# One unbroken TensorE run for two attention tiles, and stores issued by ScalarE, in a fused attention and two-layer FFN kernel

## The chip, the cores and the metric

One core of one Trainium2 chip runs the whole program. The metric is the device time of the program in microseconds (us), the median of three runs. TensorE (PE in the profile) multiplies, VectorE (DVE), ScalarE (ACT) and GpSimd (POOL) work on elements, SyncE (SP) issues transfers. A transfer is issued by an instruction of one engine's queue and then runs on the core's 16 DMA engines.

## The reference

Three stages follow each other. Lengths: 4 sequences of 768 tokens, 8 heads of 64, so 3072 tokens of width 512.

```
for c in range(768 // 32):                       # chunks of 32 queries
    k_ctx = k[32c-16 : 32c+40], clipped;  k_full = [8 memory keys, k_ctx];  the same for v
    a = softmax(q_c @ k_full.T / 8)              # the maximum is subtracted, 1e-9 added to the sum
    out_c = a @ v_full
x = out as 3072 x 512
h = x @ w_in;  g = h - tanh(h);                      x = g @ w_out     # first FFN, 512 -> 2048 -> 512
h = x @ w_in;  g = max(h, 0) + alpha * min(h, 0);  out = g @ w_out     # second FFN
```

The FFN weights arrive as 64-bit floats, everything else as 32-bit.

## The kernel before, in words

**Tiles, blocks and slots.** The 3072 tokens are 24 tiles of 128. Each FFN layer goes through 6 blocks of 4 tiles (512 columns), and each block through 16 slots, one for each 128 of the 2048 inner features. A slot is 24 matmuls of 128x512: twelve that make `h` (`emit_h`, L173) and twelve that add to the four `y` banks (`emit_y`; L212 in the first layer, L217 in the second). Twelve, since every operand is held as a high and a low part and three of the four products are taken. Between the two stands `emit_g`: in the first layer a tanh on ScalarE (L188), a subtraction on VectorE (L189), the high part on ScalarE (L197) and the low part on GpSimd (L198). TensorE works ahead: `h` of later slots is multiplied before `y` of this one.

**Attention inside the first layer.** The first five tiles get their scores before the first block, and their values mostly there too. Each later tile goes through its steps between the FFN matmuls of the first layer: `emit_scores` (16 matmuls into the bank `sp`, L301, then maximum, subtraction, exponential), `emit_soft` (sum, division, transposition, copies into `ebuf`), `tok_c`, which calls `emit_pv` (16 matmuls of `ebuf` with the values `vn` into the bank `pv`, L353, then two copies into `ring`, from where the FFN reads its input). The trace has two records for each of these 16 matmuls, so 32 for a tile's scores and 32 for its values. A dictionary `plan` sets at which half slot of which block each step is emitted: position 2f before `emit_y` of slot f, 2f+1 after it. `SPACE`, `PERIOD`, `LC`, `LP` and `SLACK` shape it. So scores of tile 5 stand at position 8 of block 0, those of tiles 6, 7 and 8 at 14, 21 and 33, and a tile's values five positions behind its scores.

**Who decides the order.** The program gives every step as an instruction stream, and a scheduler then reorders instructions on each engine, by its own model, as long as dependencies hold. `tc.issue_after(ins)` adds one edge: what is emitted under it stays behind `ins` on that engine. Before the change, only single places have such an edge. The scheduler therefore cuts the runs of `sp` and `pv` matmuls and puts FFN matmuls between the pieces.

**Buffers.** PSUM has four banks for `y`, two for `h` and two (`ps_a`) that `sp`, `pv` and the weight conversion `u` share. In SBUF, four buffers `t` are shared by tanh results, converted weights `s` and the block's results `ys`; `kbuf`, `qn` and `vn` have one buffer each for a later tile.

**Block 0 and the weights.** In block 0 each slot also converts two weight matrices of the first layer from 64 to 32 bits (`to_f32`: ScalarE L96, VectorE L99, L102, L106) and splits them. In blocks 1 to 4 the second layer's weights are converted and written to DRAM (`park`), and in block 5 they are read back (`unpark`), all by transfers that SyncE issues.

**Block ends.** `evac_y` copies the four `y` banks into four buffers `ys`, two copies by ScalarE (L233) and two by VectorE (L235), and issues four stores to `y1d` (first layer) or `out` (second), before the change all on SyncE's queue (L236). Since `ys` takes all four `t` buffers, the next tanh waits until a store has landed.

Of the kernel before, what the change touches and what calls it, by code (L numbers as in the profile page):

```python
# [17 lines left out]
L_CTX, R_CTX, CH, NM, SEQ = 16, 8, 32, 8, 768  # L18
NEG = -1.0e30
PERIOD = 20  # L20
LC, LP, SLACK = 5, 3, 2
SPACE = 6
SCB = 2
FIRST = 1
# [12 lines left out]
def chunk_attention_two_ffn_kernel(  # L37
# [128 lines left out]
    def emit_h(l, b, n, f):  # L166
        wi = wts[l, f][0]
        s0 = x0[l][b]
        h = ps_h.tile([128, 512], FP32, tag="h", name="h")[:, :n * 128]
        i = 0  # L170
        for kk in range(KD):
            for a, c in PASS:
                mm = nc.tensor.matmul(  # L173
                    out=h, lhsT=wi[:, a, kk, :], rhs=ring[c][:, s0:s0 + n, kk, :],
                    start=(i == 0), stop=(i == 3 * KD - 1),
                )
                i += 1
        last["h"] = mm.ins
        hp[l, b, f] = h

    def emit_g(l, b, n, f):
# [19 lines left out]
    def emit_y(l, b, n, f):  # L201
        wo = wts[l, f][1]
        g = gs.pop((l, b, f))
        m = KD if l == 0 else n
        if f == 0:
            yp[l, b] = [ps_y.tile([128, 512], FP32, tag="y", name="y") for _ in range(m)]
        order = ((0, 0), (1, 0), (0, 1)) if l == 0 else ((0, 0), (0, 1), (1, 0))
        for a, c in order:
            for j in range(m):
                first, last = f == 0 and (a, c) == order[0], f == NF - 1 and (a, c) == order[-1]  # L210
                if l == 0:
                    nc.tensor.matmul(  # L212
                        out=yp[l, b][j][:, :n * 128], lhsT=wo[:, a, j * 128:(j + 1) * 128],
                        rhs=g[c], start=first, stop=last,
                    )
                else:
                    nc.tensor.matmul(  # L217
                        out=yp[l, b][j], lhsT=g[a][:, j * 128:(j + 1) * 128],
                        rhs=wo[:, c, :], start=first, stop=last,
                    )  # L220

    def evac_y(l, b, n, t0):
        ys = yp.pop((l, b))
        for j, y in enumerate(ys):
            if l == 0:
                s = t_p.tile([128, 512], FP32, tag="t", name="ys")[:, :n * 128]
                src, dst = y[:, :n * 128], y1d[t0:t0 + n, :, j, :].rearrange("i p c -> p i c")
                so = s.rearrange("p (i c) -> p i c", i=n)
            else:
                s = t_p.tile([128, 512], FP32, tag="t", name="ys")  # L230
                src, dst, so = y, out[(t0 + j) * 128:(t0 + j + 1) * 128, :], s
            if j % 2 == 0:
                nc.scalar.activation(out=s, in_=src, func=ACTF.Copy)  # L233
            else:
                nc.vector.tensor_copy(out=s, in_=src)  # L235
            nc.sync.dma_start(out=dst, in_=so)  # L236

    x2 = {}

# [46 lines left out]
    def load_v(t):  # L286
        if t < NS:
            vt[t] = w_p.tile([KW, 2, H * D], FP32, tag="w", name="vn")
        else:
            vt[t] = ac.tile([KW, 2, H * D], FP32, tag="v", name="vn", bufs=1)  # L290
        nc.sync.dma_start(out=vt[t], in_=v[t])
# [3 lines left out]
    def emit_scores(t):  # L295
        s = t % TPS
        kn = kt.pop(t)
        sp = ps_a.tile([128, 512], FP32, tag="a", name="sp")
        for p in range(HP):
            for c in range(4):  # L300
                nc.tensor.matmul(  # L301
                    out=sp[CH * c:CH * c + CH, 128 * p:128 * p + 128],
                    lhsT=qt[t][:, p, CH * c:CH * c + CH],
                    rhs=kn[p // 2][:, :, p % 2, c // 2, CH * (c % 2):CH * (c % 2) + W + NM],
                    start=True, stop=True,
                )
        sp = sp.rearrange("q (h n) -> q h n", h=H)
        if s == 0:
            nc.vector.memset(sp[0:CH, :, 0:L_CTX], NEG)
        if s == TPS - 1:  # L310
            nc.vector.memset(sp[128 - CH:128, :, 64 - R_CTX:64], NEG)
        sc = aw.tile([128, H, 64], FP32, tag="sc", name="sc", bufs=SCB)
        mx = aw.tile([128, H, 1], FP32, tag="mx", name="mx")
        mb = mx.to_broadcast([128, H, 64])
        if t < SUB_POOL:
            nc.scalar.activation(out=sc, in_=sp, func=ACTF.Copy)
            nc.vector.tensor_reduce(out=mx, in_=sp, op=ALU.max, axis=AX.X)
            nc.gpsimd.tensor_tensor(out=sc, in0=sc, in1=mb, op=ALU.subtract)
        else:
            nc.vector.tensor_reduce(out=mx, in_=sp, op=ALU.max, axis=AX.X)  # L320
            nc.vector.tensor_tensor(out=sc, in0=sp, in1=mb, op=ALU.subtract)
        last["exp"] = nc.scalar.activation(out=sc, in_=sc, func=ACTF.Exp, scale=scale).ins
        sm[t] = sc
# [22 lines left out]
    def emit_pv(t, slot):  # L346
        pool, tag = (ps_h, "h") if t < NS else (ps_a, "a")
        pv = pool.tile([128, 512], FP32, tag=tag, name="pv")
        for p in range(HP):
            for a in range(2):  # L350
                for j in range(2):
                    h = 2 * p + j
                    nc.tensor.matmul(  # L353
                        out=pv[D * j:D * j + D, 128 * p + 64 * a:128 * p + 64 * a + 64],
                        lhsT=vt[t][:, a, D * h:D * h + D],
                        rhs=ebuf[:, a, h, :],
                        start=True, stop=True,
                    )
        pvv = pv.rearrange("k (p n) -> k p n", p=HP)
        nc.scalar.activation(out=ring[0][:, slot], in_=pvv, func=ACTF.Copy)  # L360
        nc.vector.tensor_tensor(
            out=ring[1][:, slot], in0=pvv, in1=f32(ring[0][:, slot]), op=ALU.subtract
        )
# [21 lines left out]
    def tok_c(t):  # L385
        b, i = first_of[t]
        if t == NS:
            with tc.issue_after(last["h"]):
                emit_pv(t, x0[0][b] + i)
        else:  # L390
            emit_pv(t, x0[0][b] + i)
        if NS < t + 1 < NTILE:
            load_v(t + 1)

    slots = [(0, b, n, f) for b, n in enumerate(blocks1) for f in range(NF)]
    slots += [(1, b, n, f) for b, n in enumerate(blocks2) for f in range(NF)]
# [2 lines left out]
    if True:  # L399
# [38 lines left out]
        def release(t):  # L438
            b, i = first_of[t]
            prev = max([x for x in range(b) if not (  # L440
                x0[0][x] + blocks1[x] <= x0[0][b] + i or x0[0][x] > x0[0][b] + i)], default=None)
            return 0 if prev is None else base[prev] + 2 * NF - 1

        def per(g):
            return PERIOD / dur[min(max(0, int(g)) // (2 * NF), len(dur) - 1)]

        at = {}
        g = 1e9
        for t in reversed(range(n0 + 1, NTILE)):
            g = min(base[first_of[t][0]] - 4 - LC, g - per(g))  # L450
            at[t] = g
        pos = -4
        todo = []
        for t in range(n0 + 1, NTILE):
            lo = max(pos + (SPACE if t > n0 + 1 else 0), 0, release(t) - LC, release(t - 1) - 2)
            pos = at[t] = max(lo, int(at[t]) - SLACK)
        for t in range(n0, NTILE):
            a = at.get(t, -4)
            nxt = at.get(t + 1, 1e9)
            c = max(min(a + LC, nxt + 2), release(t), 0)  # L460
            assert c <= base[first_of[t][0]] - 3, (t, c)
            if t > n0:
                todo.append((a, 10 * t, emit_scores, t))
                todo.append((a + 2, 10 * t + 3, emit_soft, t))
            if t > n0 and t + 1 < NTILE:
                todo.append((max(a + 1, nxt - LP), 10 * t + 1, loads_to, t + 1))
            todo.append((c, 10 * t + 12, tok_c, t))
        for a, _, fn, t in sorted(todo, key=lambda x: x[:2]):
            plan.setdefault(a, []).append((fn, t))
        nc.sync.dma_start(out=alpha_sb, in_=alpha.rearrange("(k p) -> p k", p=128))  # L470
        emit_h(*slots[0])
        emit_g(*slots[0])
        for i, (l, b, n, f) in enumerate(slots):
            def attn(pos):
                if l == 0:
                    for fn, t in plan.pop(base[b] + pos, []):
                        fn(t)

            if l == 0 and b == 0:
                more_w()  # L480
# [12 lines left out]
                if f == XF:  # L493
                    split_x2(0, blocks2[0])
            if i + 1 < len(slots):
                emit_h(*slots[i + 1])
                emit_g(*slots[i + 1])
            attn(2 * f)
            emit_y(l, b, n, f)
            if f == NF - 1:  # L500
                evac_y(l, b, n, (start1 if l == 0 else start2)[b])
            attn(2 * f + 1)
            if l == 1 and b + 1 < len(blocks2):
                if f == 2:
                    load_x2(b + 1, blocks2[b + 1], start2[b + 1])
# [63 lines left out]
```

## Time and profile before

| what | value |
|---|---|
| three runs | 1165.69, 1167.29, 1168.5 us; median 1167.29 us |
| the profiled execution | 1164.67 us, its span 1162.9 us |
| PE busy | 1125.7 us, 97% of the span |
| DVE, ACT, POOL busy | 42%, 30%, 31% |
| PE h L173, y L212, y L217 in the chain that ended last | 42%, 20%, 22% of the span |
| PE sp L301, pv L353 in that chain | 2% and 2% |

How to read it: a row of the timeline is a run of like instructions with its start, its time and the idle time before it. A matmul's record reaches past the start of the next one, because matmuls overlap; what a run takes from TensorE is therefore the time from its start to the start of the next run. A bracket at the end tells how long the engine had been idle and what it had waited for.

### The profile page before, as it was taken

Reading aid. Unit: us, or ns where it says so; the run is one execution under the profiler, and the core shown is the slowest. Engines: PE = TensorE matmul, PEld = TensorE weight load, DVE = VectorE, ACT = ScalarE, POOL = GpSimd, SP = SyncE. Lnnn points to the kernel's source line nnn. Section 1 sums busy time; section 2 is a strip of 40 time slices with the busy share of each in tenths; the row PEclk is TensorE's granted clock in tenths of the full one; section 3 lists DMA queues with packets and bytes.
Section 4 is the critical chain, followed back from the end, with each engine's and each line's share of the span. In section 5 each row is a group of like instructions: output and inputs, shape, how many; then the busy total and the mean of one; then the engine's idle time right before and its main releaser. Section 6 shows DMA issues by size and latency. Waiting matters only on the chain.

```text
span 1162.9 us, 15549 instructions
## 1 busy us (share of the span) xinstructions
PE 1125.7 (97%) x6144; PEld 914.2 (79%) x6144; DVE 488.9 (42%) x806; ACT 344.4 (30%) x612; POOL 362.9 (31%) x299
## 2 busy tenths in 40 slices
PE   3799999999999999999899999999999999999998
PEld 3587777878787777778788888888888888888886
DVE  6888645545445554454112323323323223322222
ACT  4556543434334443344222112112112112111111
POOL 4565533323333333333222222222222222222221
PEclk9799999999999999999999999999999999999999
DMA  9664244344344444335655101100101000000000
GB/s 274 221 233 143 73 144 134 123 149 128 123 145 146 133 140 149 128 123 175 221 196 186 37 1 37 37 1 37 37 1 37 37 1 1 37 1 5 33 1 36
DMA packets 53688, 112.16 MB, mean 96 GB/s; under 512 B 7280, under 2 KB 25712, under 8 KB 53616
## 3 DMA queue, kind: packets, MB, share of 16 engines
q1 hardware_dynamic: 53616, 111.18, 29.3%
q8 instruction: 48, 0.79, 0.3%
q14 instruction: 24, 0.20, 0.1%
HBM read 81.80 MB, written 29.36 MB: 96 GB/s over the span
## 4 chain that ended last, share of the span: by engine, by line
PE 89%; DVE 5%; issue 2%; DMA 2%; ACT 1%; SPq 1%; POOL 0%; DVEq 0%; POOLq 0%; ACTq 0%
PE h L173 42%; PE y L217 22%; PE y L212 20%; PE sp L301 2%; PE pv L353 2%; DVE u L102 1%; DVE s L106 1%; DVE u L99 1%; DMA w2d<-pk 1%; DMA kbuf<-in_k_dram 1%; DMA y1d<-ys 0%; DVE ebuf L344 0%; SPq L275 0%; ACT wt L112 0%; DVE et L335 0%
## 5 line engine op out<-in xcount | busy, mean ns | idle before, releaser
L173 PE MATMUL h<-ring,wt 128*128 128x512 f32 x2304 | 561.8, 392 | 12.2 <-DVE t L189 9.4
L173 PEld LDWEIGHTS h<-ring,wt 128*128 128x128 f32 x2304 | 432.1, 189 | 107.1 <-DVE t L189 11.1
L198 POOL TENSOR_TENSOR gl<-t,gh 128x512 fp32r<-128x512 f32 x192 | 248.8, 1296 | 615.6 <-ACT gh L197 585.6
L197 ACT ACTIVATE gh<-t 128x512 fp32r<-128x512 f32 x192 | 121.0, 630 | 462.3 <-DVE t L194 412.4
L191 DVE TENSOR_SCALAR t<-h,alpha_sb 128x512 f32<-128x512 f32 x96 | 72.1, 751 | 341.6 <-PE h L173 332.2
L212 PE MATMUL y<-gh,wt 128*128 128x512 f32 x768 | 195.0, 395 | 0.0
L217 PE MATMUL y<-wt,gh 128*128 128x512 f32 x768 | 191.6, 389 | 0.0
L217 PEld LDWEIGHTS y<-wt,gh 128*128 128x128 f32 x768 | 144.1, 188 | 30.0
L212 PEld LDWEIGHTS y<-gh,wt 128*128 128x128 f32 x768 | 141.6, 188 | 32.4 <-issue 2.6
L189 DVE TENSOR_TENSOR t<-h,t 128x512 f32<-128x512 f32 x96 | 66.2, 690 | 171.5 <-ACT t L188 170.9
L188 ACT ACTIVATE t<-h 128x512 f32<-128x512 f32 x96 | 57.2, 596 | 190.8 <-PE h L173 168.4
L217 PE MATMUL y<-wt,gl 128*128 128x512 f32 x384 | 104.6, 389 | 0.0
L212 PE MATMUL y<-gl,wt 128*128 128x512 f32 x384 | 103.6, 390 | 0.0
L217 PEld LDWEIGHTS y<-wt,gl 128*128 128x128 f32 x384 | 72.1, 188 | 15.0
L212 PEld LDWEIGHTS y<-gl,wt 128*128 128x128 f32 x384 | 71.9, 188 | 15.2 <-issue 0.2
L113 POOL TENSOR_TENSOR pk<-s,pk 128x512 fp32r<-128x512 f32 x32 | 41.5, 1298 | 84.7 <-ACT pk L112 84.7
L194 DVE SCALAR_TENSOR_TENSOR t<-h,t 128x512 f32<-128x512 f32 x96 | 66.4, 691 | 3.2
L99 DVE TENSOR_SCALAR u<-u 128x512 uint32<-128x512 uint32 x64 | 44.5, 696 | 27.6 <-ACT u L96 27.5
L113 POOL TENSOR_TENSOR wt<-s,wt 128x512 fp32r<-128x512 f32 x32 | 41.4, 1294 | 39.6 <-ACT wt L112 30.9
L342 ACT ACTIVATE ebuf<-et 32x256 f32<-32x256 f32 x96 | 39.8, 415 | 14.9 <-DVE et L335 13.8
L353 PEld LDWEIGHTS pv<-ebuf,vn 96*64 96x64 f32 x768 | 28.4, 148 | 19.9 <-issue 9.2
L353 PE MATMUL pv<-ebuf,vn 96*64 96x64 f32 x768 | 33.8, 237 | 7.4 <-ACT ebuf L342 6.6
(44 smaller groups left out, 485.2 us busy)
## 6 DMA issues: line engine op xcount, KB each, us to landing
w2d<-pk SPq DMA_DIRECT2D x32, 512.0 KB, 2.7
wt<-w2d SPq DMA_DIRECT2D x32, 512.0 KB, 3.6
vn<-in_v_dram SPq DMA_DIRECT2D x24, 384.0 KB, 4.0
ri<-in_moe_w_in_dram SPq DMA_DIRECT2D x16, 512.0 KB, 5.8
ro<-in_moe_w_out_dram SPq DMA_DIRECT2D x16, 512.0 KB, 6.6
pk<-in_moe_w_in_dram SPq DMA_DIRECT2D x16, 512.0 KB, 3.6
pk<-in_moe_w_out_dram SPq DMA_DIRECT2D x16, 512.0 KB, 3.6
kbuf<-in_k_dram SPq DMA_DIRECT2D x80, 96.0 KB, 2.6
```

Source lines behind the costliest of these rows:

```text
L99: nc.vector.tensor_scalar(out=u, in0=u, scalar1=3, scalar2=None, op0=ALU.logical_shift_left)
L113: nc.gpsimd.tensor_tensor(out=lo, in0=v, in1=f32(hi), op=ALU.subtract)
L173: mm = nc.tensor.matmul(out=h, lhsT=wi[:, a, kk, :], rhs=ring[c][:, s0:s0 + n, kk, :], start=(i == 0), stop=(i == 3 * KD - 1),)
L188: nc.scalar.activation(out=t, in_=h, func=ACTF.Tanh)
L189: nc.vector.tensor_tensor(out=t, in0=h, in1=t, op=ALU.subtract)
L191: nc.vector.tensor_scalar(out=t, in0=h, scalar1=0.0, scalar2=alpha_sb[:, f:f + 1], op0=ALU.min, op1=ALU.mult)
L194: nc.vector.scalar_tensor_tensor(out=t, in0=h, scalar=0.0, in1=t, op0=ALU.max, op1=ALU.add)
L197: nc.scalar.activation(out=gh, in_=t, func=ACTF.Copy)
L198: nc.gpsimd.tensor_tensor(out=gl, in0=t, in1=f32(gh), op=ALU.subtract)
L212: nc.tensor.matmul(out=yp[l, b][j][:, :n * 128], lhsT=wo[:, a, j * 128:(j + 1) * 128], rhs=g[c], start=first, stop=last,)
L217: nc.tensor.matmul(out=yp[l, b][j], lhsT=g[a][:, j * 128:(j + 1) * 128], rhs=wo[:, c, :], start=first, stop=last,)
L353: nc.tensor.matmul(out=pv[D * j:D * j + D, 128 * p + 64 * a:128 * p + 64 * a + 64], lhsT=vt[t][:, a, D * h:D * h + D], rhs=ebuf[:, a, h, : ...
```

## The change

Three things. First, `tok_c` of tile t-1 and `emit_scores` of tile t are now one step, `both(t)`. With `issue_after` edges the value matmuls stand behind the last FFN matmul emitted, the score matmuls behind the last value matmul, and the FFN matmuls that are emitted next (`emit_y` or `emit_h`) behind the last score matmul. Second, the plan has new positions: scores of tile 5 at position 2 of block 0; then value and score runs at 14, 20 and 27 of block 0, at 7, 14, 20 and 27 of blocks 1 to 3, at 7, 14 and 20 of block 4; the last tile's values alone at 26 of block 4. Third, the first layer's stores to `y1d` are issued by ScalarE instead of SyncE.

```diff
@@ emit_h, emit_y: the last FFN matmul is remembered
-                mm = nc.tensor.matmul(
+                last["ffn"] = nc.tensor.matmul(
...
+        last["ffn"] = mm.ins
@@ evac_y
-            nc.sync.dma_start(out=dst, in_=so)
+            (nc.scalar if l == 0 else nc.sync).dma_start(out=dst, in_=so)
@@ emit_scores and emit_pv: the last attention matmul is remembered
-                nc.tensor.matmul(
+                last["at"] = nc.tensor.matmul(
...
+    def behind(ins, fn, *args):
+        if ins is None:
+            return fn(*args)
+        with tc.issue_after(ins):
+            fn(*args)
+
+    def both(t):
+        behind(last["ffn"], tok_c, t - 1)
+        if t < NTILE:
+            behind(last["at"], emit_scores, t)
+        last["run"] = last["at"]
@@ the plan
+            if t == n0 + 1:
+                todo.append((release(n0), 10 * t - 9, tok_c, n0))
                 todo.append((a, 10 * t, emit_scores, t))
+            else:
+                todo.append((a, 10 * t, both, t))
...
-            todo.append((c, 10 * t + 12, tok_c, t))
@@ the loop over slots
             if i + 1 < len(slots):
-                emit_h(*slots[i + 1])
+                behind(run, emit_h, *slots[i + 1])
                 emit_g(*slots[i + 1])
-            attn(2 * f)
-            emit_y(l, b, n, f)
+            behind(attn(2 * f), emit_y, l, b, n, f)
...
-            attn(2 * f + 1)
+            run = attn(2 * f + 1)
```

What this does to TensorE's order is seen at one tile in the fourth block. Before, a tile's values (L353) and the next tile's scores (L301) stand in pieces among the matmuls of `h` and `y`:

```order
698 L173 MATMUL h<-ring_112,wt 128x512
699 L353 MATMUL pv<-ebuf,vn 64x64 x2
700 L301 MATMUL sp<-kbuf_123,qn 32x128
701 L173 MATMUL h<-ring_112,wt 128x512
702 L173 MATMUL h<-ring_113,wt 128x512
703 L353 MATMUL pv<-ebuf,vn 64x64
704 L212 MATMUL y<-gh,wt 128x512 x8
705 L353 MATMUL pv<-ebuf,vn 64x64 x2
706 L212 MATMUL y<-gl,wt 128x512 x4
707 L353 MATMUL pv<-ebuf,vn 64x64 x11
708 L173 MATMUL h<-ring_112,wt 128x512 x2
```

Here the values are in four pieces, and the first piece of scores is in front of three of them. After the change the same engine has, in that part of the program:

```order
477 L173 MATMUL h<-ring_112,wt 128x512
478 L354 MATMUL pv<-ebuf,vn 64x64 x16
479 L302 MATMUL sp<-kbuf_123,qn 32x128 x8
480 L302 MATMUL sp<-kbuf_124,qn 32x128 x8
481 L212 MATMUL y<-gh,wt 128x512 x8
482 L212 MATMUL y<-gl,wt 128x512 x4
483 L173 MATMUL h<-ring_112,wt 128x512
```

Sixteen value matmuls are followed by sixteen score matmuls with nothing between. Over the whole stretch in which FFN and attention mix, from the first `y` matmul on, the order before has 32 runs of values and 29 of scores, in 58 groups that have FFN matmuls on both sides; the order after has 20 and 19 runs, in 21 groups.

The second place is ScalarE at a block's end. Before, the two copies into `ys` are followed at once by the next tanh (L188):

```order
186 L197 ACTIVATE gh<-t 128x512
187 L188 ACTIVATE t<-h 128x512
188 L197 ACTIVATE gh<-t 128x512
189 L233 ACTIVATE ys<-y 128x512 x2
190 L188 ACTIVATE t<-h 128x512
191 L197 ACTIVATE gh<-t 128x512
```

After, the four stores stand between them on ScalarE:

```order
190 L197 ACTIVATE gh<-t 128x512
191 L96 ACTIVATE u<-pk 128x512
192 L234 ACTIVATE ys<-y 128x512 x2
193 L237 DMA y1d<-ys 128x4x128 x4
194 L188 ACTIVATE t<-h 128x512
195 L197 ACTIVATE gh<-t 128x512
```

The tanh has moved behind four transfers that are issued, and a piece of weight conversion (L96) has moved in front of the copies.

## Rows read from the trace of the kernel before

**Rows 1.** The page's share of the chain that ended last, by engine.

```profile
PE 89%; DVE 5%; issue 2%; DMA 2%; ACT 1%; SPq 1%; POOL 0%; DVEq 0%; POOLq 0%; ACTq 0%
```

**Rows 2.** Windows: stretch, length, busy us (x instructions) of engines, PE clock, DMA.

```profile
50.00:75.00 25.00, 24.78 (x134) 20.07 (x135) 21.84 (x36) 17.46 (x32) 19.74 (x16) 1.00 0.48 185
150.00:250.00 100.00, 100.00 (x642) 79.64 (x641) 50.27 (x88) 40.42 (x75) 35.55 (x29) 1.00 0.43 137
```

**Rows 3.** Timeline of PE: start, us, line, operation, [idle before <-releaser]; five separate places.

```profile
50.22 3.02 PE L173 MATMUL h<-ring,wt 128*128 128x512 f32 x12 [2.14 <-DVE t L189]
...
60.20 5.60 PE L173 MATMUL h<-ring,wt 128*128 128x512 f32 x24
65.64 0.62 PE L212 MATMUL y<-gh,wt 128*128 128x512 f32 x2
...
558.66 3.02 PE L173 MATMUL h<-ring,wt 128*128 128x512 f32 x12 [3.18 <-DVE t L189]
...
639.94 3.34 PE L173 MATMUL h<-ring,wt 128*128 128x512 f32 x14
```

**Rows 4.** Waits of PE: total us, times, longest.

```profile
PE h L173 <- DVE t L189: 9.4, 4, 3.2
```

**Rows 5.** Timeline of PE, 249 to 290 us.

```profile
249.93 1.75 PE L173 MATMUL h<-ring,wt 128*128 128x512 f32 x7
...
269.77 1.15 PE L353 MATMUL pv<-ebuf,vn 96*64 96x64 f32 x32
270.85 2.11 PE L212 MATMUL y<-gh,wt 128*128 128x512 f32 x8
272.80 1.07 PE L212 MATMUL y<-gl,wt 128*128 128x512 f32 x4
273.70 2.88 PE L173 MATMUL h<-ring,wt 128*128 128x512 f32 x12
276.51 1.08 PE L301 MATMUL sp<-kbuf,qn 128*32 128x128 f32 x32
277.52 2.11 PE L212 MATMUL y<-gh,wt 128*128 128x512 f32 x8
...
289.54 0.33 PE L353 MATMUL pv<-ebuf,vn 96*64 96x64 f32 x2
289.79 2.11 PE L212 MATMUL y<-gh,wt 128*128 128x512 f32 x8
```

**Rows 6.** Timeline of PE, 133 to 135 us.

```profile
133.82 0.34 PE L353 MATMUL pv<-ebuf,vn 96*64 96x64 f32 x4
134.09 0.41 PE L301 MATMUL sp<-kbuf,qn 128*32 128x128 f32 x2
134.42 1.04 PE L353 MATMUL pv<-ebuf,vn 96*64 96x64 f32 x28
```

**Rows 7.** Line L236: issue ns min/median/max; who waited (us, times); landing us.

```profile
L236 SPq DMA_DIRECT2D y1d<-ys x24: 370/460/1970, 149.9 to 643.2; - x24
...
  ACT t L188: 13.2, 5
...
DMA to landing us min/median/max: 2.0/2.7/6.2
```

**Rows 8.** Timeline of ACT and DVE at the end of the second block.

```profile
249.45 1.11 ACT L233 ACTIVATE ys<-y 128x512 f32<-128x512 f32 x2 [1.63 <-PE y L212]
252.55 0.60 ACT L188 ACTIVATE t<-h 128x512 f32<-128x512 f32 x1 [1.99 <-DMA y1d<-ys]
...
253.18 0.69 DVE L189 TENSOR_TENSOR t<-h,t 128x512 f32<-128x512 f32 x1 [2.15 <-ACT t L188]
```

**Rows 9.** Timeline of SP at the ends of the second and fifth block.

```profile
250.07 2.29 SPq L236 DMA_DIRECT2D y1d<-ys  x4
...
551.49 3.54 SPq L236 DMA_DIRECT2D y1d<-ys  x4
```

**Rows 10.** Timeline of ACT at the end of the fifth block.

```profile
557.28 0.60 ACT L188 ACTIVATE t<-h 128x512 f32<-128x512 f32 x1 [6.78 <-DMA y1d<-ys]
```

More of the change, by code (lines that the diff above doesn't have):

```diff
@@ L20 @@
 PERIOD = 20
-LC, LP, SLACK = 5, 3, 2
+LP, SLACK, LAST_C = 3, 2, 5
 SPACE = 6
@@ L172, in emit_h @@
             for a, c in PASS:
-                mm = nc.tensor.matmul(
+                last["ffn"] = nc.tensor.matmul(
                     out=h, lhsT=wi[:, a, kk, :], rhs=ring[c][:, s0:s0 + n, kk, :],
                     start=(i == 0), stop=(i == 3 * KD - 1),
-                )
+                ).ins
                 i += 1
-        last["h"] = mm.ins
+        last["h"] = last["ffn"]
         hp[l, b, f] = h
@@ L209, in emit_y @@
             for j in range(m):
-                first, last = f == 0 and (a, c) == order[0], f == NF - 1 and (a, c) == order[-1]
+                first, final = f == 0 and (a, c) == order[0], f == NF - 1 and (a, c) == order[-1]
                 if l == 0:
-                    nc.tensor.matmul(
+                    mm = nc.tensor.matmul(
                         out=yp[l, b][j][:, :n * 128], lhsT=wo[:, a, j * 128:(j + 1) * 128],
-                        rhs=g[c], start=first, stop=last,
+                        rhs=g[c], start=first, stop=final,
                     )
                 else:
-                    nc.tensor.matmul(
+                    mm = nc.tensor.matmul(
                         out=yp[l, b][j], lhsT=g[a][:, j * 128:(j + 1) * 128],
-                        rhs=wo[:, c, :], start=first, stop=last,
+                        rhs=wo[:, c, :], start=first, stop=final,
                     )
+        last["ffn"] = mm.ins
     def evac_y(l, b, n, t0):
@@ L300, in emit_scores @@
             for c in range(4):
-                nc.tensor.matmul(
+                last["at"] = nc.tensor.matmul(
                     out=sp[CH * c:CH * c + CH, 128 * p:128 * p + 128],
@@ L305, in emit_scores @@
                     start=True, stop=True,
-                )
+                ).ins
         sp = sp.rearrange("q (h n) -> q h n", h=H)
@@ L352, in emit_pv @@
                     h = 2 * p + j
-                    nc.tensor.matmul(
+                    last["at"] = nc.tensor.matmul(
                         out=pv[D * j:D * j + D, 128 * p + 64 * a:128 * p + 64 * a + 64],
@@ L357, in emit_pv @@
                         start=True, stop=True,
-                    )
+                    ).ins
         pvv = pv.rearrange("k (p n) -> k p n", p=HP)
@@ L448, in chunk_attention_two_ffn_kernel @@
         g = 1e9
-        for t in reversed(range(n0 + 1, NTILE)):
-            g = min(base[first_of[t][0]] - 4 - LC, g - per(g))
+        for t in reversed(range(n0 + 2, NTILE + 1)):
+            g = min(base[first_of[t - 1][0]] - 3, g - (per(g) if t < NTILE else 0))
             at[t] = g
+        todo = []
         pos = -4
[L453 to L462, printed above, removed]
+        for t in range(n0 + 1, NTILE + 1):
+            if t == n0 + 1:
+                pos = 2
+            else:
+                lo = max(pos + SPACE, release(t - 1))
+                pos = max(lo, int(at[t]) - SLACK)
+                if t == NTILE:
+                    pos = max(lo, min(pos, at[t - 1] + LAST_C))
+            at[t] = pos
+            assert t == n0 + 1 or pos <= base[first_of[t - 1][0]] - 3, (t, pos)
+        for t in range(n0 + 1, NTILE + 1):
+            a, nxt = at[t], at.get(t + 1, 1e9)
+            if t == n0 + 1:
+                todo.append((release(n0), 10 * t - 9, tok_c, n0))
                 todo.append((a, 10 * t, emit_scores, t))
+            else:
+                todo.append((a, 10 * t, both, t))
+            if t < NTILE:
                 todo.append((a + 2, 10 * t + 3, emit_soft, t))
-            if t > n0 and t + 1 < NTILE:
+            if t + 1 < NTILE:
                 todo.append((max(a + 1, nxt - LP), 10 * t + 1, loads_to, t + 1))
-            todo.append((c, 10 * t + 12, tok_c, t))
         for a, _, fn, t in sorted(todo, key=lambda x: x[:2]):
@@ L472, in chunk_attention_two_ffn_kernel @@
         emit_g(*slots[0])
+        run = None
         for i, (l, b, n, f) in enumerate(slots):
@@ L477, in attn @@
                         fn(t)
+                    return last.pop("run", None)
             if l == 0 and b == 0:
```

## The prediction

> **What bounds the kernel now.** I read the chain of waits first: 89% of what ended last is TensorE's own work, 2% are DMA, 5% VectorE [rows 1]. The windows come next. In a steady stretch, 150 to 250 us, TensorE is busy 100.00 of 100 us at clock 1.00, while VectorE, ScalarE and GpSimd are busy 50, 40 and 36 us [rows 2]. Block 0 differs: from 50 to 75 us VectorE is busy 21.84 of 25 us, since it converts weights there [rows 2]. So nearly everywhere only fewer or cheaper TensorE instructions help, and in block 0 VectorE is the second bound.
>
> Next the timeline of TensorE, for what the attention costs in the first layer. An undisturbed pair of `h`, 24 matmuls, takes 5.44 us from start to next start (60.20 to 65.64), or 0.2267 us each [rows 3]. From the first `h` after the start-up to the first `h` of the second layer, 50.22 to 639.94, pass 589.72 us [rows 3]. Six blocks of 16 slots of 24 are 2304 matmuls, 522.2 us at that pace. Of the other 67.5 us, TensorE waits some: the view of waits has 9.4 us in 4 waits for the subtraction L189 [rows 4]; 2.14 lie ahead of 50.22 and 3.18 ahead of 558.66 [rows 3], so 4.1 belong to the other two, 2.04 each, both in block 0. That makes 7.3, and leaves 60.2 us for attention between FFN matmuls: values of 20 tiles, scores of 19.
>
> **What a run and a border cost.** Start to next start again. Values: two records take 0.25 us (289.54), 32 take 1.08 (269.77): 0.028 each and 0.195 fixed [rows 5]. Scores: two take 0.33 (134.09), 32 take 1.01 (276.51): 0.023 each and 0.285 fixed [rows 5, 6]. Beside this, the twelve `h` ahead of a run take 2.81 us (273.70 to 276.51) and not 2.72: 0.09. The eight `y` behind one take 1.95 (270.85 to 272.80) and not 1.81: 0.14. So a border pair with the FFN costs 0.23 [rows 5].
>
> These prices rebuild the total: 32 runs of values, 29 of scores, 58 groups give 6.2 + 8.3 + 13.3 fixed, and 640 + 608 records give 17.7 + 13.8; 59.3 us against the 60.2 measured. The model holds to 1 us.
>
> **The change part by part.** (1) Runs no longer cut: 32 to 20 and 29 to 19. 12 x 0.195 + 10 x 0.285 = 5.2 us less. (2) 58 groups to 21: 37 x 0.23 = 8.5 us less. Together 13.7. All of it lies on TensorE, which bounds this stretch, so it counts in full unless a new wait takes it. Is the passage from values straight to scores as cheap as I take it, its fixed 0.285 and nothing for a border? At 133.82 the old order has that passage by chance: four value records 0.27, then two scores 0.33 [rows 6], where the prices without a border give 0.31 and 0.33. So the cheap end of the passage is seen; the dear end is a full 0.23 each, 18 x 0.23 = 4.1 us, which leaves 9.6. I take 13.7, by the row.
>
> (3) New order on the other engines, blocks 1 to 4. A run joined to 2.1 us pushes `y` or `h` behind it back by 1 us more than a single run did; but softmax of a tile and the tanh chain sit on engines that are half idle there [rows 2], and a tile's values now have six or seven half slots, over 16 us, from its scores. I cost this at nothing; the cover is that idle half. Values waiting for `ebuf` would now hold the whole of TensorE, since nothing may pass them: at the head of TensorE's queue a late softmax costs its full delay.
>
> (4) Block 0. Tile 8's scores move from its last position (33) to 27, and both `ps_a` banks must be free for a joined run, while VectorE has 3.2 of 25 us left. Bounds: both old waits go, -4.1; or scores of 5 to 8, four bursts, each cost one wait of 2.04, that is 8.2 and +4.1 net. I take +2.5, nearer the upper end, because of VectorE's 21.84.
>
> (5) Stores on ScalarE. At the end of the second block ScalarE's copies end at 250.56 [rows 8]; SyncE issued from 250.07, four in 2.29 us [rows 9]; tanh started at 252.55, when a store had landed, and the subtraction ended at 253.87 [rows 8]. Issued by ScalarE after its own copies, the stores begin 0.49 later, hold it until 252.85 at SyncE's price, and the landing, 2.48 after the first issue, comes at 253.04; subtraction done about 254.36. TensorE starts its next `h` at 249.93 [rows 5]; with 24 matmuls ahead of the bank that this subtraction frees, it needs it at 255.37. One us is left, in which a landing of more than the median 2.7 [rows 7] can come late. Behind the issues on ScalarE wait tanh and the high part, and behind them GpSimd and TensorE. Bounds over the four ends of blocks 0 to 3 and that of block 5: 0 to 5 x 3.2, the worst old one; I take 1.5 in all, near the median landing.
>
> (6) The end of block 4. There SyncE was still issuing reads of parked weights; the stores were issued at 551.49, tanh started at 557.28 after 6.78 us [rows 9, 10], and TensorE lost 3.18 [rows 3]. ScalarE can issue about 1 us earlier, at 550.5. If transfers only queue for the DMA engines, the landing gains that 1 us; if they stood behind SyncE's own queue, the landing takes some 2.0 to 2.7 [rows 7], and all 3.18 go. I take 2.0 saved.
>
> The Trainium skill, DMA: Bandwidth & Descriptors, section Issuing engines are not separate DMA queues, says that transfers of all issuers run on the same 16 DMA engines, and another issuer saves only issue time. By it this step gives 1 us, and the whole sum 10.7. No row of before tells which.
>
> **Sum.** -13.7 + 2.5 + 1.5 - 2.0 = -11.7 us. The profiled execution took 1164.67 (its span of 1162.9 and 1.8 around it, which nothing here touches), so it would be 1153.0; it lies 2.6 below the median 1167.29, and the same step from the median gives 1155.6 us.
>
> **Rivals.**
> A, the forecast. For it: attention's fixed parts, 27.8 us, are seen in rows, and TensorE is never short of work in the steady stretch. Own range 1151 to 1160: from step 6 whole and no loss in block 0, -13.7 - 3.2 + 0.5 = -16.4, to the dear passage, -9.6 + 2.5 + 1.5 - 2.0 = -7.6. Chance 62%.
> B, VectorE becomes the bound of block 0, and block ends cost their share: two waits of 2.04 at each of the four bursts, +12.2 net, with -13.7, +1.5 and -2.0: -2.0, about 1165; half as bad, -6, about 1161. For it: 21.84 of 25. Against: before, two waits only in all of block 0. Chance 18%, most of it at 1161.
> C, better than forecast: old waits in block 0 vanish as the run leaves VectorE longer stretches, -13.7 - 4.1 + 1 - 3.2 = -20, 1147. Against: tile 8's scores are now in block 0. Chance 9%.
> D, slower: the stores hold ScalarE. SyncE's longest issue took 1.97 us [rows 7]; four like it are 7.9 us, so at the second block's end tanh starts at 258.4 and the subtraction ends at 259.8, 4.4 after TensorE needs it; at six ends that is 26 us, against -11.2 of steps 1, 2 and 4, so +15, 1182. It decides from 1.9 us lost per end, an issue of some 1.4 us. Against: the median is 0.46. Chance 6%.
> E, the order doesn't matter: the fixed cost is per tile and a run is only moved, or late softmax at the head of TensorE's queue takes back 0.65 us at each of the 18 runs, 11.7 in all. 1167. Against: pieces of two records cost 0.25 and 0.33 where their share is 0.06. Chance 5%.
>
> **How the numbers follow.** Predicted is A, 1155.6. The range 1149 to 1163 holds A, the milder B and part of C, some 81%. A difference under 0.2%, 2.3 us, can't be told from none. Faster than that: A, C, most of B (15%): 86%. Same: the bad end of B and most of E: 7%. Slower: D and a part of E: 7%.
>
> **What the profile after would show.** Runs of 32 value records directly followed by 32 score records, start to start 1.08 and 1.0, and 21 groups; if the second takes 1.25 the passage is dear. TensorE's time from 50 to the first second-layer `h` shorter by 10 to 14 us, net of waits. Waits for L189 in block 0 of 4 to 9 us (B: over 10). At block ends stores issued by ScalarE within 2.5 us, and tanh no later than 1 us after before; D if they take 5. At the fifth end, a wait of 0 to 2.2 instead of 3.18. Waits of value matmuls for `ebuf` in steady blocks would prove step 3 wrong, and slower `h` and `y` matmuls beside the runs, or a granted clock below 1.00 there, the prices.

## The result and the profile after

The changed kernel takes 1150.9 us (median of 4 runs, 1149.64 to 1151.61), the kernel before 1166.63 in the same count of runs: 15.7 us less, a ratio of 0.9862 with the 95% interval 0.9845 to 0.9879. The forecast was 11.7 less. The profiled execution took 1150.37 us with a span of 1148.5, so 14.3 us less than the profiled one of before (its span is 14.4 less); what follows divides those.

The chain that ended last is still TensorE's, as in [rows 1]:

```profile
PE 88%; DMA 4%; DVE 3%; issue 2%; SPq 1%; POOL 1%; ACT 0%; DVEq 0%; POOLq 0%; ACTq 0%
```

The timeline of TensorE shows one joined run, in the place that answers to [rows 5]:

```profile
288.46 1.75 PE L173 MATMUL h<-ring,wt 128*128 128x512 f32 x7
290.14 1.15 PE L354 MATMUL pv<-ebuf,vn 96*64 96x64 f32 x32
291.22 1.08 PE L302 MATMUL sp<-kbuf,qn 128*32 128x128 f32 x32
292.23 2.11 PE L212 MATMUL y<-gh,wt 128*128 128x512 f32 x8
294.18 1.08 PE L212 MATMUL y<-gl,wt 128*128 128x512 f32 x4
```

From start to start the values take 1.08 and the scores 1.01 us, as much as each takes alone in [rows 5]; the eight `y` behind them take 1.95, once for both. The stretch that [rows 3] bound, and the waits in it, look like this:

```profile
50.65 3.01 PE L173 MATMUL h<-ring,wt 128*128 128x512 f32 x12 [1.94 <-DVE t L189]
...
105.78 3.02 PE L173 MATMUL h<-ring,wt 128*128 128x512 f32 x12 [0.64 <-DVE t L189]
...
113.77 4.61 PE L173 MATMUL h<-ring,wt 128*128 128x512 f32 x12 [2.25 <-DVE t L189]
...
448.67 3.02 PE L173 MATMUL h<-ring,wt 128*128 128x512 f32 x12 [0.68 <-DVE t L189]
...
544.83 3.02 PE L173 MATMUL h<-ring,wt 128*128 128x512 f32 x12 [0.51 <-DVE t L189]
...
626.11 3.34 PE L173 MATMUL h<-ring,wt 128*128 128x512 f32 x14
```

50.65 to 626.11 are 575.46 us, against 589.72 before. Less 522.2 for 2304 matmuls, 53.2 remain; 4.08 of them are the four waits that begin after 50.65. The twelve `h` at 113.77 show something new: 4.61 us instead of 3.02. The windows say why (columns as in [rows 2]):

```profile
112.00:113.70 1.70, 0.00 (x0) 0.00 (x0) 1.70 (x4) 1.15 (x2) 0.44 (x1) 1.00 0.00 0
...
114.00:118.00 4.00, 4.00 (x12) 3.09 (x11) 2.91 (x5) 2.72 (x5) 3.86 (x4) 0.57 0.00 0
...
550.00:643.00 93.00, 93.00 (x412) 77.04 (x411) 17.68 (x26) 20.75 (x35) 22.29 (x17) 1.00 0.52 166
```

TensorE did nothing from 112.0 to 113.7, and from 114 to 118 its granted clock was 0.57 on average, mostly the lower level of 1.2 GHz: 4.00 x 0.43 = 1.7 us lost. Attention is then 53.2 - 4.1 - 1.7 = 47.4 us, against 60.2 before. The price list of the prediction has 45.6 for 20 and 19 runs in 21 groups.

Where they went, by place: attention -12.8; waits in block 0, 4.07 before and 0.64 + 2.25 after, -1.2; half clock behind the second of them +1.7; a new wait at the fourth block's end +0.7; the fifth block's end, 3.18 before and 0.51 after, -2.7. The stretches ahead of the first row and behind the last give +0.4 and -0.6.

At the block ends the stores are ScalarE's now. Line and queue, in the form of [rows 7], then ScalarE at the second, fourth and fifth end, as [rows 8 to 10]:

```profile
L237 ACTq DMA_DIRECT2D y1d<-ys x24: 367/465/1807, 152.5 to 628.9; - x24
...
  ACT t L188: 15.0, 6
...
DMA to landing us min/median/max: 2.0/2.7/7.5
```

```profile
248.93 1.11 ACT L234 ACTIVATE ys<-y 128x512 f32<-128x512 f32 x2 [0.16 <-PE y L212]
...
249.41 3.11 PE L173 MATMUL h<-ring,wt 128*128 128x512 f32 x13
...
249.80 2.31 ACTq L237 DMA_DIRECT2D y1d<-ys  x4
...
252.24 0.60 ACT L188 ACTIVATE t<-h 128x512 f32<-128x512 f32 x1 [2.21 <-DMA y1d<-ys]
...
442.38 2.88 PE L173 MATMUL h<-ring,wt 128*128 128x512 f32 x12
443.63 0.62 ACT L96 ACTIVATE u<-pk 128x512 f32<-128x512 f32 x1 [2.75 <-DMA pk<-in_moe_w_out_dram]
444.28 1.09 ACT L234 ACTIVATE ys<-y 128x512 f32<-128x512 f32 x2
444.91 2.30 ACTq L237 DMA_DIRECT2D y1d<-ys  x4
...
538.72 2.88 PE L173 MATMUL h<-ring,wt 128*128 128x512 f32 x12
538.87 2.29 ACTq L237 DMA_DIRECT2D y1d<-ys  x4
...
543.45 0.60 ACT L188 ACTIVATE t<-h 128x512 f32<-128x512 f32 x1 [4.10 <-DMA y1d<-ys]
```

The issue costs the same median on either engine, 0.46 us. The `h` that follows the block's last `y` marks the end of the block on TensorE. At the second end the issue begins 0.39 us behind the start of that `h`; SyncE's began 0.14 behind it. At the fifth, it begins 0.15 behind instead of 1.61. At the fourth it begins 2.53 behind, 0.14 before: a piece of weight conversion (L96) stands ahead of the copies on ScalarE and waited 2.75 us for its transfer, so the copies begin 1.90 behind that `h`. This is where the new wait of 0.68 us stands.

### The profile page after: what moved, and what is told of

Its sections match the earlier page's. It is cut to its first block, busy times and chain, and to the rows that moved or that the text cites. A ratio compares the mean times of both kernels' runs of the same rounds, so it can differ in the third digit from the quotient of the medians.

```text
span 1148.5 us, 15553 instructions
## 1 busy us (share of the span) xinstructions
PE 1114.7 (97%) x6144; PEld 915.6 (80%) x6144; DVE 485.5 (42%) x806; ACT 345.5 (30%) x612; POOL 363.1 (32%) x299
## 4 chain that ended last, share of the span: by engine, by line
PE 88%; DMA 4%; DVE 3%; issue 2%; SPq 1%; POOL 1%; ACT 0%; DVEq 0%; POOLq 0%; ACTq 0%
PE h L173 42%; PE y L217 23%; PE y L212 20%; PE pv L354 2%; PE sp L302 1%; DMA ri<-in_moe_w_in_dram 1%; DMA alpha_sb<-in_moe_alpha_dram 1%; DVE u L102 1%; DMA y1d<-ys 1%; SPq L276 1%; DVE s L106 1%; DVE u L99 1%; DVE ebuf L345 0%; DMA vn<-in_v_dram 0%; DMA w2d<-pk 0%
## 5 line engine op out<-in xcount | busy, mean ns | idle before, releaser
L188 ACT ACTIVATE t<-h 128x512 f32<-128x512 f32 x96 | 57.1, 595 | 184.9 <-PE h L173 169.2
L212 PEld LDWEIGHTS y<-gl,wt 128*128 128x128 f32 x384 | 72.0, 188 | 15.7 <-POOL gl L198 0.4
L345 DVE COPY ebuf<-et 32x256 f32<-32x256 f32 x96 | 39.0, 407 | 1.8
```

Of the source, the lines that this page charges most:

```text
L188: nc.scalar.activation(out=t, in_=h, func=ACTF.Tanh)
L212: mm = nc.tensor.matmul(out=yp[l, b][j][:, :n * 128], lhsT=wo[:, a, j * 128:(j + 1) * 128], rhs=g[c], start=first, stop=final,)
```

## The experiments

Theory 1 is the prediction's: TensorE pays for each run and each border with the FFN, and the change has fewer. Its rivals: the stores carry the gain, the plan's new positions do, or joining adds nothing to keeping runs whole. Attention in the table is the same subtraction as above (from the first `h` behind the start-up to the first of the second layer, less 2304 x 0.2267, less waits, less busy time x (1 - clock) in 2 us windows). Two profiles of the same kernel differ by up to 0.5 us in it (47.4 and 46.9, the changed kernel and e8). Runs and groups are counted in the trace over the same stretch; from the first `y` matmul on, where the section on the change starts its counts, there is one run of values and one group fewer in each kernel.

| kernel | median us | ratio to before, 95% | attention | waits | half clock | runs of values, scores, groups |
|---|---|---|---|---|---|---|
| before | 1166.63 | 1 | 60.2 | 7.3 | 0 | 32, 29, 58 |
| changed | 1150.9 | 0.9862 (0.9845 to 0.9879) | 47.4 | 4.1 | 1.7 | 20, 19, 21 |
| e1 joined, stores on SyncE | 1153.4 | 0.988 (0.9854 to 0.9905) | 47.3 | 5.4 | 3.3 | 20, 19, 21 |
| e2 stores alone | 1165.09 | 0.9976 (0.996 to 0.9992) | 60.7 | 6.0 | 1.5 | 32, 29, 58 |
| e3 whole runs, old plan | 1158.26 | 0.9905 (0.9873 to 0.9937) | 51.4 | 6.3 | 4.2 | 22, 19, 41 |
| e4 new plan, no edges | 1157.66 | 0.991 (0.9887 to 0.9934) | 52.1 | 5.5 | 1.6 | 30, 20, 32 |
| e5 scores apart | 1151.11 | 0.9856 (0.9824 to 0.9889) | 50.3 | 4.6 | 1.6 | 20, 19, 39 |
| e6 copies on ScalarE | 1150.23 | 0.9843 (0.981 to 0.9876) | 47.5 | 3.9 | 0 | 20, 19, 22 |
| e7 copies on GpSimd | 1148.49 | 0.983 (0.9798 to 0.9862) | 47.0 | 1.3 | 1.6 | 20, 19, 22 |
| e8 changed, again | 1151.43 | 0.9845 (0.9818 to 0.9872) | 46.9 | 3.7 | 3.4 | 20, 19, 21 |
| e9 = e5 again | 1153.38 | 0.986 (0.9838 to 0.9883) | 50.1 | 1.9 | 1.7 | 20, 19, 39 |
| e10 = e7 again | 1147.14 | 0.9812 (0.979 to 0.9834) | 46.9 | 1.5 | 1.7 | 20, 19, 22 |
| e11 e5 and e7 | 1150.75 | 0.9845 (0.9818 to 0.9873) | 50.2 | 1.5 | 0 | 20, 19, 39 |

The kernels of one group (e1 to e4, e5 to e7, e8 to e11) were timed beside each other. The kernel before had medians of 1168.06, 1168.67 and 1168.92 us there.

**e1, the joined runs without the stores.**

```diff
-            (nc.scalar if l == 0 else nc.sync).dma_start(out=dst, in_=so)
+            nc.sync.dma_start(out=dst, in_=so)
```

> The changed kernel with the first layer's stores back on SyncE; the joined runs and the new plan stay. Theory 1 (TensorE's runs and borders): most of the gain stays; only the fifth block's end goes back from a wait of 0.5 us to about 3.2, so some 12.5 to 13 us faster than before and 2.7 slower than the changed kernel. Rival (the stores carry the gain): less than half, under 7 us faster than before.

14.7 us faster than the 1168.06 beside it, some 2 us more than expected, with the expected 12.5 to 13 inside the interval (11.1 to 17.1). The wait at the fifth end is back at 2.46 us, attention the same as in the changed kernel. The rival that the stores carry the gain falls.

**e2, the stores without the joined runs.**

```diff
-            nc.sync.dma_start(out=dst, in_=so)
+            (nc.scalar if l == 0 else nc.sync).dma_start(out=dst, in_=so)
```

> The kernel before with only the first layer's stores moved to ScalarE. Theory 1: 2 to 3.5 us faster, all of it at the fifth block's end (TensorE's wait of 3.18 us there shrinks to about 0.5), attention runs as before with 60 us between FFN matmuls. Rival (the stores carry the gain): more than 8 us faster. Rival (ScalarE held by the issues): slower, with tanh later at each block's end.

3.0 us faster by medians, as expected, with an interval of 0.9 to 4.7. The fifth end gives only part of it: its wait is 1.96 us, 1.2 less than before. ScalarE and TensorE there:

```profile
551.96 2.88 PE L173 MATMUL h<-ring,wt 128*128 128x512 f32 x12
552.10 2.43 ACTq L236 DMA_DIRECT2D y1d<-ys  x4
...
558.14 0.60 ACT L188 ACTIVATE t<-h 128x512 f32<-128x512 f32 x1 [5.55 <-DMA y1d<-ys]
...
559.52 2.79 PE L173 MATMUL h<-ring,wt 128*128 128x512 f32 x11 [1.96 <-DVE t L189]
```

The issue is 1.5 us earlier against the last `y`, but from there to the tanh, which waits for the first landing, it takes 6.0 us; before, 5.8. So in this pair the other queue saved the issue's delay and nothing of the transfer. That is what the Trainium skill, DMA: Bandwidth & Descriptors, section Issuing engines are not separate DMA queues, states, and this trace agrees: 1.5 us of issue, 1.2 us of wait. Over all profiles, SyncE issues 1.35 to 2.60 us behind the last `y` at the fifth end (three profiles) and ScalarE 0.15 (all ten), while the time from issue to tanh is 5.3 to 5.8 us on SyncE and 4.0 to 6.8 on ScalarE (4.6 in the changed kernel). So the earlier issue is shown, a faster transfer is not, and why the transfer varies was not tried. The rest of e2's 3 us does not appear as a wait of TensorE in its profile, which at 1165.75 us is no faster than the one of before (1164.67), and stays open.

**e3, whole runs, but not joined.** Old plan and stores; the change's order edges around each run.

```diff
+    def whole(fn, t):
+        behind(last["ffn"], fn, t)
+        last["run"] = last["at"]
...
-                todo.append((a, 10 * t, emit_scores, t))
+                todo.append((a, 10 * t, lambda t: whole(emit_scores, t), t))
...
-            todo.append((c, 10 * t + 12, tok_c, t))
+            todo.append((c, 10 * t + 12, (lambda t: whole(tok_c, t)) if t > n0 else tok_c, t))
```

> The kernel before, its plan and its stores, with order edges alone: each run of values and each run of scores is whole, but they are not joined to each other. Its order has 22 runs of values, 19 of scores in 41 groups. Theory 1 by the prices 0.195, 0.285 and 0.23: 2.0 + 2.9 + 3.9 = 8.7 us off attention, so 8 to 9 us faster if no wait is added. Rival (cutting costs little, only joining pays): under 4 us. Rival (the edges cost waits, since nothing may pass a late run): same or slower, with waits of TensorE for ebuf or L189.

9.8 us faster. In the trace attention falls by 8.9, for 8.7 by the prices. The profiled execution was the slowest of the four, 1161.96: the first `h` behind the start-up comes 3.2 us later than before, and its fifth end cost 3.98 us and then half clock. The other three were not profiled.

```profile
53.38 4.61 PE L173 MATMUL h<-ring,wt 128*128 128x512 f32 x12 [2.86 <-DVE t L189]
...
553.72 5.40 PE L173 MATMUL h<-ring,wt 128*128 128x512 f32 x12 [3.98 <-DVE t L189]
...
637.46 3.34 PE L173 MATMUL h<-ring,wt 128*128 128x512 f32 x14
```

```profile
550.00:552.00 2.00, 0.00 (x0) 0.00 (x0) 0.00 (x0) 0.00 (x0) 0.00 (x0) 1.00 1.12 337
...
554.00:558.00 4.00, 4.00 (x10) 3.14 (x11) 0.44 (x1) 0.96 (x2) 2.52 (x2) 0.50 0.40 151
```

The edges also showed their price here: values waited 1.82 us for `ebuf` in block 0, at the head of TensorE's queue. The rival that edges only add waits falls, since the sum is still 10 us, and so does the rival that only joining pays.

**e4, the new plan without the edges.**

```diff
-        if ins is None:
-            return fn(*args)
-        with tc.issue_after(ins):
-            fn(*args)
+        fn(*args)
```

> The changed kernel with its plan and stores but without the order edges: the scheduler is free to cut. Its order has 30 runs of values, 20 of scores in 32 groups. Theory 1: 10 x 0.195 + 1 x 0.285 + 11 x 0.23 = 4.8 us more attention than the changed kernel, so about 11 us faster than before. Rival (the edges are what matters): about the time of before less 3. Rival (the new positions are what matters): the time of the changed kernel, within 1 us.

10.4 us faster, as expected; the changed kernel is some 5 us better. So two thirds of the gain come with the plan and the stores, because at these positions the scheduler itself leaves most scores whole and beside values (32 groups instead of 58), and the edges bring the last third. Neither rival as put holds: the positions act through the number of groups. From the first `h` behind the start-up (53.16) to the first of the second layer (634.57), attention is 52.1 us, 4.7 more than in the changed kernel where the prices say 4.8. The price list itself (50.4) is 1.7 too low here, as it is 1.8 too low for the changed kernel; no kernel of the table lies further above it.

**e5 and e9, scores half a slot behind the values.**

```diff
         behind(last["ffn"], tok_c, t - 1)
-        if t < NTILE:
-            behind(last["at"], emit_scores, t)
         last["run"] = last["at"]
...
+    def scores(t):
+        behind(last["ffn"], emit_scores, t)
+        last["run"] = last["at"]
...
                 todo.append((a, 10 * t, both, t))
+                if t < NTILE:
+                    todo.append((a + 1, 10 * t - 5, scores, t))
```

> The changed kernel with whole runs and its plan and stores, but a tile's scores one half slot behind the values instead of directly behind: 38 groups where the changed kernel has 20, the same number of runs. It prices the passage from values to scores. Theory 1 (a passage has no border with the FFN, 0.23 us): 18 x 0.23 = 4.1 us slower than the changed kernel, 11.5 faster than before. Rival (the passage costs as much as a border): the time of the changed kernel, within 1 us.

Timed against before, e5 was level with the changed kernel, 1151.11, where 4.1 us slower had been expected. But the trace had 50.3 us of attention, 2.9 more. Both were therefore timed beside each other, and without block 0's waits (e11).

> The changed kernel once more, on the chip and in the rounds of the kernels beside it. All theories: 15 to 16 us faster than before.

> Whole runs with the scores a half slot behind the values, as before, now timed beside the changed kernel. The trace of its first run has 3.0 us more attention than the changed kernel, while its times were level. Theory 1 (a border less is worth what the trace says): 2 to 4 us slower than the changed kernel, unless block 0 gives back the 2.9 us of waits and 1.8 of half clock. Rival (joining is worth nothing): level within 1 us.

The changed kernel is 17.5 us faster than before in these rounds, above the expected 15 to 16. 1153.38 against 1151.43: apart is 2.0 us slower, though the five runs of each overlap (1152.53 to 1153.67 and 1150.1 to 1153.69), and the traces of e8 and e9 give 3.2 us more attention, of which smaller waits (1.9 for 3.7) and less half clock (1.7 for 3.4) give back 3.5; outside the stretch e9's profile is 2.4 us longer (start-up 1.3, the rest 1.1), which the edit does not explain. So the 2.0 by time are no clean price of the passage. The trace of e9:

```profile
291.20 0.39 PE L173 MATMUL h<-ring,wt 128*128 128x512 f32 x1
291.51 1.15 PE L354 MATMUL pv<-ebuf,vn 96*64 96x64 f32 x32
292.60 2.11 PE L212 MATMUL y<-gh,wt 128*128 128x512 f32 x8
294.54 1.07 PE L212 MATMUL y<-gl,wt 128*128 128x512 f32 x4
295.54 1.08 PE L302 MATMUL sp<-kbuf,qn 128*32 128x128 f32 x32
296.55 3.01 PE L173 MATMUL h<-ring,wt 128*128 128x512 f32 x12
```

The runs take what they take when joined, 1.09 and 1.01, and each has its own border: eight `y` in 1.94 instead of 1.81, twelve `h` in 2.85 instead of 2.72.

**e6, e7 and e10, copies of block 0's tiles off VectorE.** Four of the eight copies into `ebuf` go to ScalarE (e6) or GpSimd (e7, e10) for tiles 5 to 8.

```diff
-            if i < ACT_COPIES:
+            if i < (8 if NS < t < 9 else ACT_COPIES):      # e6
...
-                nc.vector.tensor_copy(out=o, in_=src)
+                (nc.gpsimd if NS < t < 9 else nc.vector).tensor_copy(out=o, in_=src)      # e7, e10
```

> The changed kernel with all eight copies into ebuf on ScalarE for tiles 5 to 8, the tiles of block 0, where VectorE has four of them. Theory (VectorE's queue makes the waits of block 0, 0.64 + 2.25 us, and the clock that falls to half behind the second, 1.8 us): these go, up to 4.7 us faster than the changed kernel, 1146 to 1149. Rival (ScalarE's queue, which holds the tanh behind its copies): the waits stay or grow, 1151 or more.

> The same four copies of tiles 5 to 8 moved from VectorE to GpSimd, ScalarE as in the changed kernel. Theory (VectorE's queue): the waits of 0.64 + 2.25 us in block 0 and the 1.8 us of half clock go, 1146 to 1149. Rival (ScalarE's queue): the waits stay, 1151. Rival (GpSimd becomes late with the low part): waits of the y matmuls for GpSimd, 1151 or more.

> The changed kernel with four ebuf copies of tiles 5 to 8 on GpSimd, timed beside the others. Theory (VectorE's queue made block 0's waits and the half clock): 3 to 4.5 us faster than the changed kernel. Rival: the first time was luck, level within 1 us.

In the changed kernel VectorE had, ahead of the wait of 2.25 us:

```profile
107.57 2.90 DVE L345 COPY ebuf<-et 32x256 f32<-32x256 f32 x4
...
113.03 0.68 DVE L189 TENSOR_TENSOR t<-h,t 128x512 f32<-128x512 f32 x1
```

In e10 GpSimd does the copies, in 1.70 us, and VectorE comes to the same subtraction earlier; TensorE's only wait there is a short one:

```profile
109.84 1.70 POOL L345 COPY ebuf<-et 32x256 f32<-32x256 f32 x4
```

```profile
107.14 3.06 PE L173 MATMUL h<-ring,wt 128*128 128x512 f32 x12 [0.41 <-DVE t L189]
...
111.54 0.69 DVE L189 TENSOR_TENSOR t<-h,t 128x512 f32<-128x512 f32 x1
```

e10 is 4.3 us faster than the changed kernel beside it, 1147.14 for 1151.43, the best of all kernels here, 0.9812 of before. The traces of e8 and e10 differ by 2.2 us of waits and 1.7 of half clock, with the same attention. VectorE's queue is shown as the cause of the wait of 2.25 us and of the half clock behind it; the half clock that e10 still has stands behind the start-up. The third rival, GpSimd late with the low part, shows as a wait of 0.17 us.

Why four copies held VectorE for 2.90 us is in the same trace: the shortest took 0.29, the longest 1.28, and two instructions of GpSimd ran beside them.

```profile
L345 DVE COPY ebuf<-et x4: 287/644/1284, 107.6 to 110.2; 32x256 f32<-32x256 f32 x4
...
107.13 1.29 POOL L198 TENSOR_TENSOR gl<-t,gh 128x512 fp32r<-128x512 f32 x1
108.39 1.34 POOL L113 TENSOR_TENSOR wt<-s,wt 128x512 fp32r<-128x512 f32 x1
```

The first two copies, of 1.00 and 1.28 us, each ended 0.14 to 0.15 us behind one of these two; the other two took 0.29 each. On ScalarE, e6, the time is level with the changed kernel (1150.23), since the copies only move the wait: the tanh stands behind them.

```profile
126.79 3.41 ACT L343 ACTIVATE ebuf<-et 32x256 f32<-32x256 f32 x8 [0.78 <-DVE et L336]
...
130.23 0.60 ACT L188 ACTIVATE t<-h 128x512 f32<-128x512 f32 x1
...
132.05 2.11 PE L212 MATMUL y<-gh,wt 128*128 128x512 f32 x8 [2.12 <-ACT gh L197]
```

**e11, both.**

> Both edits: scores a half slot behind the values, and the copies of tiles 5 to 8 on GpSimd, so that block 0's waits are small in both this kernel and the one with the copies alone, and the passage is priced without them. Theory 1: 3 to 4 us slower than the changed kernel with the copies. Rival (joining is worth nothing): level with it within 1 us.

1150.75, 3.6 us slower than e10, and no run of e11 (1148.8 to 1155.72) is as fast as any of e10 (1146.81 to 1148.73). With the same 1.5 us of waits in both, the trace gives 50.2 less 46.9, 3.3 us more attention. The rival that joining is worth nothing falls. That 3.6 and 3.3 agree so closely is in part luck: e10's profile has 1.7 us of half clock from the start-up that e11's lacks, and e11's is 1.6 longer outside the stretch, which the edit does not explain.

## Why the prediction was right

**Steps 1 and 2, fewer runs and borders, -13.7.** Measured -12.8 in the trace, and the experiments bear it out piece by piece: whole runs alone -8.9 (e3, 8.7 by the prices), passages -2.9 to -3.3 (e5, e9, e11, 4.1 by the prices). The passage is cheap, as the prediction took it. Its row of before showed less than it says, though: the price of two scores, 0.33 us, was read from that same row, so only the four values, 0.27 for 0.31, were a test. A border pair that is taken away by joining is worth 3.1 / 18 = 0.17 us, not 0.23, and over 18 passages that is 1.1 us, enough for the 0.9 missing of the 13.7. The rows read 128*128, 96*64 and 128*32 for FFN, values and scores, and the Trainium skill, TensorEngine Tiling (Array Packing), section Key Properties, says that changing the tiling mode drains TensorE; the trace agrees in so far as each return to the FFN has its price and the scores keep their fixed part inside a joined run. That the draining is what costs it, no run here shows.

**Step 3, nothing in blocks 1 to 4.** Right: no value run waits for `ebuf` behind 50 us in the changed kernel.

**Step 4, block 0, +2.5.** The waits, which are all that the step sums, did not grow but fell, from 4.07 to 2.89; the waits of 4 to 9 us that it expected there did not come. The half clock behind one of them, which the prediction put at nothing, added 1.7, and so the block lost 0.5 after all: that it came out as a loss is luck. The reason given, a VectorE that is nearly full, was right for the wait that is left (e10).

**Step 5, the block ends, +1.5.** Too dear: +0.7, one wait. The issue at the second end is later by 0.25 us, half of the 0.49 forecast, and costs nothing there. The one wait, at the fourth end, has a cause that the step does not name: the conversion L96 in front of ScalarE's copies. It is not the queue of the stores, since e1, with the stores on SyncE, also issues 0.74 and 1.40 us behind the last `y` at the third and fourth end. In e8, the changed kernel again, L96 waited 1.51 us instead of 2.75 there, and TensorE did not wait at all.

**Step 6, the fifth end, -2.0.** Measured -2.7 in the profiled pair. Over all profiles the wait there is 2.46 to 3.98 with stores on SyncE and 0 to 2.76 on ScalarE, so that a single pair says little about it. The means are 3.2 of three and 1.1 of ten, so 2.1 saved, as forecast; the smaller price, 1 us, was what e2 showed. The mean delay of SyncE's issue, 1.9 us against ScalarE's 0.15, is enough for it without a faster transfer.

Together: the gains of 15.7 (steps 1, 2 and 6) became 15.5, and the losses of 4.0 became 1.2: 14.3 where 11.7 were forecast. The steps mis-sized are the two losses. The medians say 15.7, with an interval of about 14 to 18; the 1.4 between are not in any row. The time of 1150.9 us lies inside the stated range, at the lower edge of the forecast's own, 1151 to 1160. Rivals B, D and E are out (the milder B is mis-summed: half of 12.2 makes -8, not -6, which changes nothing here); C is half right, since block 0 lost little, but not because its waits vanished.

## What to carry to other kernels

Where TensorE is the bound, count the runs of small matmuls and the returns to the large ones, price each from start-to-start times of two run lengths, and join them; the price list from the trace of before held to 0.9 us in 13.7 here. What shares an engine with the chain that TensorE waits for (copies, softmax, conversions) can be worth more moved to another engine than the matmuls that remain to be joined: 4.3 us for four copies of each of four tiles. The other engine need not be idle, since GpSimd was busy 19.74 of 25 us in block 0 before [rows 2]; what counts is that the tanh and the subtraction do not stand behind the copies there. A kernel that pays twice for a wait, in time and then in clock, gives both back when the wait goes.

## What the runs showed of the hardware beyond that

TensorE's clock fell to 0.50, 1.2 GHz, behind some waits and not behind others: behind 2.25 us in block 0 in the changed kernel, e1, e4 and e8, behind 2.76 in e5, 2.86 and 3.98 in e3, and in six more profiles behind the last wait of the start-up (2.34 to 3.08), but not behind 2.08, 1.99 and 3.18 in the kernel before, nor 2.46 at the fifth end of e1. Each fall cost 1.5 to 2.6 us. The length of the wait alone does not decide it; what does was not tried.

Copies on VectorE waited for GpSimd. In the changed kernel VectorE makes 96 copies of 32x256 into `ebuf`. The 80 that began with no GpSimd instruction running took 0.28 to 0.29 us. The 16 that began while one ran took 0.34 to 1.29 us, and each ended 0.14 to 0.15 us behind the end of that instruction. GpSimd itself took 0.39 for such a copy in e10 (1.70 for four), so it is not the faster engine.
